# State products of three weight chunks in two row halves of the array, the first two reads in column groups, and a late store issued by ScalarE

## The chip, the cores and the metric

The kernel runs on one core of one Trainium2 chip. The metric is the device time of one execution in microseconds (us), as the median of several runs. The page and the trace come from one profiled execution.

## What is computed

Eight batches of attention against a small state (8 heads, 512 tokens, 32 state rows, width 64) are followed by two feed-forward layers. Cut to what matters:

```python
scores = x @ state.T / 8                 # a = softmax over the 32 state rows
xread  = softmax(scores, -1) @ state     # 512 rows for each batch and head
sread  = softmax(scores.T, -1) @ x       # 32 rows for each batch and head
x = concat(xread, sread)                 # 8 x (512 + 32) rows of width 512
g = relu(x @ w_in) ** 2                  # w_in 512 x 2048
x = g @ w_out                            # w_out 2048 x 512
h = x @ w2_in                            # then h * softmax(h), a layer norm, and @ w2_out
```

Everything is worked out in float32 to about its precision. A factor is split into a high and a low part, both in 32 bits, and a product is three matmuls: high by high, high by low, low by high.

## The kernel before

`xread` is never formed for the first layer. Since xread @ w_in = softmax @ (state @ w_in), the kernel forms **state products**: for each batch the rows state @ w_in (32 state rows of 8 heads, in four chunks of 512 columns of w_in). The hidden layer of a batch is then softmax times those rows (`hidden`, two triples of matmuls for 128 hidden columns), `project` accumulates the second product in four PSUM banks, and ScalarE and VectorE square and split between them.

The state products come in three kinds. Chunk 0 of batches 0 and 1 goes straight from PSUM into a tile (`sw_direct`). Chunk 0 of batches 2 and 3, and chunks 1 to 3 of batches 0 to 3, are made by `sw_part(u, j)`: u is chunk times 4 plus the pair of heads, j the pair of batches. Its weights hold one head of two batches, in `bdw` for j = 0 and `bd` for j = 1; the other head's rows of these 128 rows are zeros, so a pair of heads and two batches fill 128 columns, and three matmuls make them (`triple`, lines 149 to 151 of the profile). ScalarE copies the bank out (L347), and SyncE (SP) stores it to DRAM. `late_part` does batches 4 to 7 later (L417 and L418), with the copy L419 on ScalarE and the store L421 in SP's queue. `load_sw` fetches the rows back.

The **reads** (`sread` in the reference) are small matmuls in plain float32, each of which the trace shows as two passes. For batches 0 and 1, `sread` takes x as weights, 64 columns wide, and moves 32 columns (L651), and ScalarE puts the result into the tile `sr`. From batch 2 on `read_four` takes the softmax as weights, 32 columns wide, in four column groups of the array and moves 64 columns (L673); VectorE transposes the result (`tq`), which goes through DRAM into `sr`.

What sets the order: up to the 28th hidden block (about the first 170 us) the order of TensorE, VectorE, ScalarE and SP is a list written out by hand, `PLAN`. A letter names a kind of work and each time a name stands there one step of it is issued: W is `sw_part`, F the first reads, U a step of the state's transposes, H, G, L and P the parts of the feed-forward. GpSimd follows its own order. After that `step` places the work block by block (16 blocks for a batch), with tables `tensor`, `scalar`, `vector` and `after` for the attention of the batch after next, and a table `EARLY` at the turn to the second layer. All PSUM banks of `ps_m` (two, for transposes, scores and most state products) and of `ps_h` (two, for `hidden`) are taken in turn.

## Time and profile before

| | |
|---|---|
| Median of 3 runs | 1025.05 us (1024.75 to 1026.1) |
| The profiled execution's own time | 1025.25 us |
| Its span, first to last instruction | 1023.5 us |
| TensorE busy | 1007.6 us (98%) |
| VectorE busy | 780.6 us (76%) |
| ScalarE busy | 624.1 us (61%) |
| GpSimd busy | 135.4 us (13%) |

A timeline row gives an instruction's start, its duration, engine, line, output, inputs and shape, and in brackets the idle time of its engine before it with what ended it. A matmul's duration holds its way through the array, so the pace of TensorE is read from start to start and not from durations.

### The profile page before, as it was taken

How to read it: one execution, taken by the hardware profiler on the slowest of the kernel's cores; microseconds unless marked ns; L12 is line 12 of the kernel's file. 1: busy time of each engine (PE TensorE's matmuls, PEld its weight loads, DVE VectorE, ACT ScalarE, POOL GpSimd, SP SyncE). 2: the span in 40 equal slices, each digit the busy share in tenths (PEclk: the TensorE clock that was granted, in tenths of full speed). 3: DMA queues.
4: the chain of work that ended last, by engine and by line, in shares of the span. 5: the costliest groups of instructions: out<-in, count | busy, mean ns of one | idle time of the engine just before them, and what ended most of it. 6: DMA issues, size and time to landing. Idle time of an engine off the chain costs nothing.

```text
span 1023.5 us, 14984 instructions
## 1 busy us (share of the span) xinstructions
PE 1007.6 (98%) x5118; PEld 837.4 (82%) x5118; DVE 780.6 (76%) x1383; ACT 624.1 (61%) x1047; POOL 135.4 (13%) x170
## 2 busy tenths in 40 slices
PE   6999999999999999999999999999999999999998
PEld 4788888888888878888888889998888888888887
DVE  7999889788677588697796455699788788778861
ACT  6998776466566555465564443476756666666652
POOL 1000000001000000010000023322422332232010
PEclk9999999999999999999999999999999999999999
DMA  9788976687787773543542726444355445444431
GB/s 250 294 251 266 303 241 205 195 231 200 220 233 221 205 206 106 157 119 113 150 114 90 214 62 203 147 144 160 130 177 166 141 152 177 155 139 159 154 114 53
DMA packets 193837, 179.53 MB, mean 175 GB/s; under 512 B 103008, under 2 KB 142944, under 8 KB 193760
## 3 DMA queue, kind: packets, MB, share of 16 engines
q1 hardware_dynamic: 193040, 178.31, 57.1%
q8 instruction: 40, 0.66, 0.2%
q14 instruction: 37, 0.30, 0.1%
q10 hardware_dynamic: 720, 0.26, 0.1%
HBM read 109.45 MB, written 69.07 MB: 174 GB/s over the span
## 4 chain that ended last, share of the span: by engine, by line
PE 90%; DVE 4%; ACT 2%; DMA 2%; issue 1%; SPq 0%; ACTq 0%; DVEq 0%
PE b L1065 14%; PE acc L149 11%; PE acc L150 11%; PE acc L151 11%; PE ps_h L149 6%; PE ps_h L150 6%; PE ps_h L151 6%; PE ps_o L1208 6%; PE ps_o L1207 6%; PE ps_o L1206 6%; PE ps_sw L418 1%; PE ps_sw L417 1%; PE ps_sr L673 1%; DMA a_st<-in_state_dram 1%; DMA st<-in_moe_w_out_dram 1%
## 5 line engine op out<-in xcount | busy, mean ns | idle before, releaser
L149 PE MATMUL acc<-gh,w1out 128*128 128x512 f32 (+1 forms) x576 | 219.0, 380 | 0.0
L150 PE MATMUL acc<-gl,w1out 128*128 128x512 f32 (+1 forms) x576 | 217.6, 378 | 0.0
L151 PE MATMUL acc<-gh,w1out 128*128 128x512 f32 (+1 forms) x576 | 217.5, 378 | 0.0
L907 ACT ACTIVATE r<-ps_h 128x512 f32<-128x512 f32 (+1 forms) x144 | 82.5, 573 | 127.4 <-PE ps_h L151 124.9
L922 DVE TENSOR_TENSOR gl<-r,gh 128x512 fp32r<-128x512 f32 (+1 forms) x144 | 97.9, 680 | 55.3 <-ACT gh L917 49.0
L917 ACT ACTIVATE gh<-r 128x512 fp32r<-128x512 f32 (+1 forms) x144 | 87.3, 606 | 70.4 <-DVE r L911 64.0
L151 PEld LDWEIGHTS acc<-gh,w1out 128*128 128x128 f32 x576 | 108.4, 188 | 20.2
L149 PEld LDWEIGHTS acc<-gh,w1out 128*128 128x128 f32 x576 | 108.4, 188 | 20.2
L150 PEld LDWEIGHTS acc<-gl,w1out 128*128 128x128 f32 x576 | 108.4, 188 | 19.8 <-DVE gl L922 0.2
L911 DVE TENSOR_TENSOR r<-r,ps_h 128x512 f32<-128x512 f32 (+1 forms) x120 | 77.6, 646 | 45.0 <-ACT r L907 43.8
L1208 PE MATMUL ps_o<-w,ll 128*128 128x512 f32 x272 | 106.0, 390 | 0.3 <-DVE s L1121 0.3
L1206 PE MATMUL ps_o<-w,lh 128*128 128x512 f32 x272 | 106.0, 390 | 0.0
L1207 PE MATMUL ps_o<-w,lh 128*128 128x512 f32 x272 | 105.8, 389 | 0.0
L149 PE MATMUL ps_h<-ah,sw 128*128 128x512 f32 x256 | 100.1, 391 | 0.0
L150 PE MATMUL ps_h<-al,sw 128*128 128x512 f32 x256 | 99.7, 389 | 0.0
L151 PE MATMUL ps_h<-ah,sw 128*128 128x512 f32 x256 | 99.6, 389 | 0.0
L209 POOL TENSOR_TENSOR cw<-cw,ce 128x512 f32<-128x512 f32 x16 | 20.7, 1295 | 493.0 <-DVE ce L206 409.4
L1065 PE MATMUL b<-w,x2h 128*128 128x512 f32 x272 | 83.9, 390 | 0.0
L1138 POOL TENSOR_TENSOR var<-var,mhalf 128x1 f32<-128x1 f32 x34 | 35.1, 1032 | 247.3 <-DVE var L1137 247.3
L1181 ACT ACTIVATE lh<-ln_t 128x1024 fp32r<-128x1024 f32 x32 | 33.8, 1055 | 46.8 <-PE ps_o L1207 45.1
L1208 PEld LDWEIGHTS ps_o<-w,ll 128*128 128x128 f32 x272 | 51.0, 188 | 11.3 <-DVE ll L1187 0.7
L1206 PEld LDWEIGHTS ps_o<-w,lh 128*128 128x128 f32 x272 | 51.1, 188 | 10.6
(246 smaller groups left out, 2031.2 us busy)
## 6 DMA issues: line engine op xcount, KB each, us to landing
ln_d<-ln_sq SPq DMA_DIRECT2D x32, 512.0 KB, 3.4
ln_t<-ln_d SPq DMA_DIRECT2D x128, 128.0 KB, 2.9
stg<-sw_d SPq DMA_DIRECT2D x120, 128.0 KB, 3.5
sw_d<-ev_sw SPq DMA_DIRECT2D x28, 512.0 KB, 3.9
st<-in_moe_w_out_dram SPq DMA_DIRECT2D x24, 512.0 KB, 4.8
st_x<-x_d SPq DMA_DIRECT2D x34, 256.0 KB, 3.6
w1i_d<-w1in SPq DMA_DIRECT2D x16, 512.0 KB, 5.7
st<-in_moe_w_in_dram SPq DMA_DIRECT2D x16, 512.0 KB, 5.2
```

What stands on the lines that cost most here:

```text
L149: nc.tensor.matmul(out=ps, lhsT=lh, rhs=rh, start=first and i == 0, stop=False)
L150: nc.tensor.matmul(out=ps, lhsT=lh, rhs=rl, start=False, stop=False)
L151: nc.tensor.matmul(out=ps, lhsT=ll, rhs=rh, start=False, stop=last and i == n - 1)
L907: nc.scalar.activation(out=r, in_=ps, func=AF.Relu)
L911: nc.vector.tensor_tensor(out=r, in0=r, in1=ps, op=ALU.mult)
L917: nc.scalar.activation(out=gh, in_=r, func=AF.Copy if times else AF.Square)
L922: nc.vector.tensor_tensor(out=gl, in0=r, in1=gh.bitcast(F32), op=ALU.subtract)
L1065: nc.tensor.matmul(out=ps, lhsT=l, rhs=r, start=first and k == 0 and j == 0, stop=k == 1 and j == 2, skip_group_check=True,)
L1138: nc.gpsimd.tensor_tensor(out=var, in0=var, in1=mhalf, op=ALU.pow)
L1206: nc.tensor.matmul(out=ps, lhsT=a, rhs=wt[:, 0, o : o + 512], start=(k == 0), stop=False)
L1207: nc.tensor.matmul(out=ps, lhsT=a, rhs=wt[:, 1, o : o + 512], start=False, stop=False)
L1208: nc.tensor.matmul(out=ps, lhsT=bb, rhs=wt[:, 0, o : o + 512], start=False, stop=(k == NK - 1))
```

## The change

Three edits of substance, with the orders written anew around them.

First, for chunks 1 to 3 a new `sw_rows` makes the products of one pair of heads for all four batches. A new tile `stw` holds the state of one head in partitions 0 to 63 and of the other head in 64 to 127, four batches in 128 columns. Two matmuls of 64 rows, one in each row half of the array, go to two PSUM banks, one of `ps_m` and one of `ps_h`; three such pairs make the product. Sixteen copies by GpSimd fill `stw` from `bdw` and `bd`. Chunk 0 of batches 2 and 3 stays as it was, and is stored in two pieces. The stores go to one tensor `sw1_d` in place of four. `stw` uses the buffer of `sr`, which is taken later.

Second, batches 0 and 1 are read by `read_four` too, through the transpose and DRAM.

Third, the store of `late_part` is issued by ScalarE.

Beside that: `PLAN` is another list; the columns' softmax of batches 3 to 7 and the reads of all batches from 2 on stand one step earlier; the fetched softmax uses the buffers `xh` and `xl`; the entry 22 of `EARLY` puts `part_hi` ahead of `sol_square`.

```diff
+    stw = srp.tile([P, 2, NQ, 2, 2, 2 * NS], F32R, tag="sr", name="stw")
...
+        if t > 1:
+            return
+        for l in range(2):
+            o, n = slice(l * D, (l + 1) * D), slice(l * NS, (l + 1) * NS)
+            for i in range(2):
+                for lo in range(2):
+                    nc.gpsimd.tensor_copy(
+                        out=stw[o, lo, :, i, t].rearrange("p q (n b) -> p q n b", b=2),
+                        in_=half(i, lo)[o, :, n, :],
+                    )
...
+        if c:
+            yield from sw_rows(c, hp, t)
+            return
...
+    def sw_rows(c, hp, t):
+
+        q, i = divmod(hp, 2)
+        pss = [bank("ps_sw"), ps_h.tile([P, 512], F32, tag="h", name="ps_sw")]
+        for n, (lo, r) in enumerate(((0, 0), (0, 1), (1, 0))):
+            for l in range(2):
+                o = slice(l * D, (l + 1) * D)
+                nc.tensor.matmul(
+                    out=pss[l],
+                    lhsT=stw[o, lo, q, i].rearrange("p j r -> p (j r)"),
+                    rhs=t[o, r, :],
+                    start=(n == 0),
+                    stop=(n == 2),
+                    tile_position=(l * D, 0),
+                )
+        ev = evp.tile([P, 2, 512], F32, tag="ev", name="ev_sw")
+        for l in range(2):
+            yield 1
+            nc.scalar.activation(out=ev[:, l, :], in_=pss[l], func=AF.Copy)
+        yield 1
+        nc.sync.dma_start(out=sw1_d[:, 2 * hp : 2 * hp + 2, c * FC : (c + 1) * FC], in_=ev)
...
         if i == 1:
-            nc.sync.dma_start(out=sw2_d[:, 2 * k : 2 * k + 2, c * FC : (c + 1) * FC], in_=ev)
+            nc.scalar.dma_start(out=sw2_d[:, 2 * k : 2 * k + 2, c * FC : (c + 1) * FC], in_=ev)
...
+        def read_four(i):
...
+            for t in range(NT):
+                for hp in range(NHP):
+                    h = 2 * hp + i
+                    nc.tensor.matmul(
+                        out=v["ps_sr"][hp * NS : (hp + 1) * NS, i * D : (i + 1) * D],
+                        lhsT=col_of(t, h),
+                        rhs=xs_t[b][:, t, h, :] if b < 2 else xs[:, h // 4, t, h % 4, :],
...
+                        tile_position=(0, hp * NS),
+                    )
...
-        after = {14: [(read_four,), (read_turn,)]}
+        after = {13: [(read_four, 0), (read_four, 1), (read_turn,)]}
...
-    I2 i2 I0 X0 i2 U0 i0 U0 i2 X0 i0 i2 X0 U0 i0 i0 i2 X0 T02 T03 i0 i0 T00 J0 J2 i2 U0 T02 N02 i2 T03 T00
+    I2 I0 X0 X0 X0 X0 i2 J0 i0 U0 i0 U0 T02 T03 i0 i0 i0 i2 i2 J2 i0 U0 T02 i0 i2 T03 X1 U0 i2 T00 N02 i0 X1
...
-        22: ([(sol_square, 2, "A")], [(part_hi, 1, "A"), (part_lo, 1, "A"), (sol_mul, 2, "B"), (load_pair, 5)]),
+        22: ([(part_hi, 1, "A")], [(part_lo, 1, "A"), (sol_square, 2, "A"), (sol_mul, 2, "B"), (load_pair, 5)]),
```

TensorE at the first products of chunk 1. Before, one product of a pair of heads is two triples, each into a bank of its own; `bdw_221` holds batches 0 and 1, `bd1_1_204` batches 2 and 3.

```order
L149 MATMUL ps_sw_697<-w1in_605,bdw_221 128x512
L150 MATMUL ps_sw_697<-w1in_605,bdw_221 128x512
L151 MATMUL ps_sw_697<-w1in_605,bdw_221 128x512
L149 MATMUL ps_sw_708<-w1in_605,bd1_1_204 128x512
L150 MATMUL ps_sw_708<-w1in_605,bd1_1_204 128x512
L151 MATMUL ps_sw_708<-w1in_605,bd1_1_204 128x512
L149 MATMUL acc3_713<-gh_616,w1out_382 128x512
```

TensorE at the first product of chunk 1 now: the two banks alternate, and the rows of `project` stand on either side.

```order
L402 MATMUL ps_sd_634<-sw_690,negi_199 128x512
L372 MATMUL ps_sw_701<-w1in_434,stw_206 128x512
L372 MATMUL ps_sw_702<-w1in_434,stw_206 128x512
L372 MATMUL ps_sw_701<-w1in_434,stw_206 128x512
L372 MATMUL ps_sw_702<-w1in_434,stw_206 128x512
L372 MATMUL ps_sw_701<-w1in_434,stw_206 128x512
L372 MATMUL ps_sw_702<-w1in_434,stw_206 128x512
L156 MATMUL acc2_712<-gh_667,w1out_386 128x512
```

Six rows stay six, with half the rows of the array each, and they make what six made before.

SP before, at a store of `late_part` (`sw2_d`) between loads of x for the attention (`xs`), of a late product's weights (`w1in`) and of state products (`stg`):

```order
L517 DMA xs_208<-in_x_dram 32x16x32 x8
L274 DMA w2_d3_69<-cw_3877 128x512
L401 DMA w1in_4097<-w1i_d3_65 64x2x512 x2
L421 DMA sw2_d_61<-ev_sw_4132 128x2x512
L439 DMA stg_4148<-sw2_d_61 32x2x512 x4
L687 DMA sr_d4_125<-tq_3989 128x128
```

SP now at the same place, without the store:

```order
L546 DMA xs_207<-in_x_dram 32x16x32 x8
L281 DMA w2_d3_66<-cw_3909 128x512
L434 DMA w1in_4129<-w1i_d3_62 64x2x512 x2
L469 DMA stg_4180<-sw2_d_58 32x2x512 x4
L693 DMA sr_d4_124<-tq_3976 128x128
```

The store now stands on ScalarE, behind the two copies that fill its tile and ahead of the next blocks' squares:

```order
L920 ACTIVATE r_3767<-ps_h_3751 128x512
L452 ACTIVATE ev_sw_3778<-ps_sw_3779 128x512
L452 ACTIVATE ev_sw_3778<-ps_sw_3786 128x512
L454 DMA sw2_d_58<-ev_sw_3778 128x2x512
L930 ACTIVATE gh_3799<-r_3767 128x512
L920 ACTIVATE r_3821<-ps_h_3801 128x512
```

One entry has left SP's queue and joined ScalarE's, at each of the 16 late products.

ScalarE before at entry 22 of `EARLY`: the square `hA,var` stands ahead of the high part `lh` of a row of the second layer's input to w2_out.

```order
L1086 ACTIVATE s_7620<-b_7610 128x512
L1131 ACTIVATE hA,var<-e,mu 128x1024
L1181 ACTIVATE lh<-ln_t 128x1024
L1219 ACTIVATE ob<-ps_o 128x512
L1131 ACTIVATE hB,var<-e,mu 128x1024
```

ScalarE there now:

```order
L1099 ACTIVATE s_7652<-b_7642 128x512
L1194 ACTIVATE lh<-ln_t 128x1024
L1144 ACTIVATE hA,var<-e,mu 128x1024
L1232 ACTIVATE ob<-ps_o 128x512
L1144 ACTIVATE hB,var<-e,mu 128x1024
```

The square has moved behind the high part, and nothing else has moved there.

## Rows read from the trace of the kernel before

**Rows 1.** The page: span, and busy time with share of each engine.

```profile
span 1023.5 us, 14984 instructions
PE 1007.6 (98%) x5118; PEld 837.4 (82%) x5118; DVE 780.6 (76%) x1383; ACT 624.1 (61%) x1047; POOL 135.4 (13%) x170
```

**Rows 2.** Who waited for whom: total us, times, longest us.

```profile
ACT r L907 <- PE ps_h L151: 124.9, 102, 2.8
...
PE ps_st L305 <- DMA a_st<-in_state_dram: 8.9, 1, 8.9
...
PE ps_s L738 <- ACT ev_sw L419: 1.0, 2, 0.8
```

**Rows 3.** Busy time in two stretches: us of each engine (instructions), clock, DMA.

```profile
25.00:77.00 52.00, 51.45 (x297) 41.55 (x296) 50.61 (x111) 49.34 (x98) 2.10 (x2) 1.00 0.81 273
25.00:170.00 145.00, 144.00 (x763) 117.65 (x762) 132.17 (x270) 122.58 (x234) 2.10 (x2) 1.00 0.82 261
```

**Rows 4.** Instructions on the tile ps_sw: ns least/median/most, first and last start, form.

```profile
L347 ACT ACTIVATE ev_sw<-ps_sw x28: 578/597/678, 32.0 to 142.7; 128x512 f32<-128x512 f32 x28
L149 PEld LDWEIGHTS ps_sw<-w1in,bd x16: 186/188/190, 28.2 to 136.3; 128*128 128x128 f32 x16
L149 PE MATMUL ps_sw<-w1in,bd x16: 389/391/507, 28.4 to 136.6; 128*128 128x512 f32 x16
...
L149 PE MATMUL ps_sw<-w1in,bdw x12: 389/389/496, 43.0 to 139.3; 128*128 128x512 f32 x12
```

**Rows 5.** Timeline of TensorE: a product's first matmul and the one behind it.

```profile
58.61 0.39 PE L149 MATMUL ps_sw<-w1in,bdw 128*128 128x512 f32 x1
...
59.29 0.39 PE L149 MATMUL acc<-gh,w1out 128*128 128x512 f32 x1
```

**Rows 6.** Timeline of TensorE: matmuls of 256 columns, ten apart.

```profile
629.77 0.28 PE L149 MATMUL ps_h<-sh,w1in 128*128 128x256 f32 x1
...
630.98 0.28 PE L150 MATMUL ps_h<-sl,w1in 128*128 128x256 f32 x1
```

**Rows 7.** Timeline of TensorE around reads of batch 0, and a half of batch 1.

```profile
69.36 0.40 PE L151 MATMUL acc<-gh,w1out 128*128 128x512 f32 x1
69.69 2.06 PE L651 MATMUL ps_sr<-e,xs 128*64 128x32 f32 x64
...
72.01 0.39 PE L150 MATMUL ps_sw<-w1in,bdw 128*128 128x512 f32 x1
...
111.55 0.39 PE L151 MATMUL ps_h<-ah,sw 128*128 128x512 f32 x1
...
113.26 0.39 PE L150 MATMUL acc<-gl,w1out 128*128 128x512 f32 x1
```

**Rows 8.** Timeline of TensorE around the read of batch 2, in column groups.

```profile
194.92 0.39 PE L151 MATMUL ps_h<-ah,sw 128*128 128x512 f32 x1
195.24 1.10 PE L673 MATMUL ps_sr<-xs,e 128*32 128x64 f32 x64
...
196.61 0.40 PE L150 MATMUL acc<-gl,w1out 128*128 128x512 f32 x1
```

**Rows 9.** Timeline of TensorE at two of its few waits.

```profile
361.59 0.39 PE L151 MATMUL acc<-gh,w1out 128*128 128x512 f32 x1
362.76 0.50 PE L738 MATMUL ps_s<-xh,bd 128*128 128x512 f32 x1 [0.78 <-ACT ev_sw L419]
...
714.18 0.39 PE L1207 MATMUL ps_o<-w,lh 128*128 128x512 f32 x1
714.89 0.50 PE L1208 MATMUL ps_o<-w,ll 128*128 128x512 f32 x1 [0.32 <-DVE s L1121]
```

**Rows 10.** Timeline of VectorE just ahead of the second of these waits.

```profile
713.61 1.22 DVE L1187 TENSOR_TENSOR ll<-ln_t,lh 128x1024 fp32r<-128x1024 f32 x1 [0.73 <-ACT lh L1181]
```

**Rows 11.** Timeline of ScalarE's queue: two DMAs that it issues.

```profile
2.32 1.21 ACTq L294 DMA_DIRECT2D a_st<-in_state_dram  x2
```

**Rows 12.** Timeline of GpSimd: the first of its two early products.

```profile
27.09 1.05 POOL L607 TENSOR_TENSOR e<-e,sm 128x512 f32<-128x512 f32 x1 [22.46 <-DVE sm L605]
```

More of the change, by code (lines that the diff above doesn't have):

```diff
@@ L56, in memory_attention_relu2_solu @@
     dram = ctx.enter_context(tc.tile_pool(name="dram", bufs=1, space=DRAM))
-    sw_d = [dram.tile([P, B // 4, F1], F32, name=f"sw_d{hp}", tag=f"sw{hp}") for hp in range(NHP)]
+    sw1_d = dram.tile([P, H, F1], F32, name="sw1_d", tag="sw1")
     sw2_d = dram.tile([P, H, F1], F32, name="sw2_d", tag="sw2")
@@ L69, in memory_attention_relu2_solu @@
     st_d = [dram.tile([P, 2, S], F32, name=f"st_d{b}", tag=f"st{b}") for b in range(2, B)]
-    sr_d = [dram.tile([P, P], F32, name=f"sr_d{b}", tag=f"sr{b}") for b in range(2, B)]
+    sr_d = [dram.tile([P, P], F32, name=f"sr_d{b}", tag=f"sr{b}") for b in range(B)]
     x2p_d = [dram.tile([P, NM, S], F32, name=f"x2p_d{b}", tag=f"x2p_{b}") for b in range(2)]
@@ L120, in memory_attention_relu2_solu, with sr_tile @@
     bdw = {}
-    sr = srp.tile([P, NHP, NSR], F32, tag="sr", name="sr")
+    stw = srp.tile([P, 2, NQ, 2, 2, 2 * NS], F32R, tag="sr", name="stw")
+    srt = []
+    def sr_tile():
+        if not srt:
+            srt.append(srp.tile([P, NHP, NSR], F32, tag="sr", name="sr"))
+        return srt[0]
     def split(hi, lo, src):
@@ L329, in sw_part @@
         c, hp = divmod(u, NM)
-        i = hp % 2
-        single = c == 0
-        at = i if single else j
-        ps = ps_h.tile([P, 512], F32, tag="h", name="ps_sw") if u < AHEAD else bank("ps_sw")
-        if j == 0:
-            lh, ll = (bdw[0][:, i, hp // 2, k] for k in (i, 2 + i))
-        else:
-            lh, ll = (bd[i][j][:, hp // 2, k] for k in (i, 1 - i))
-        lh, ll = lh.rearrange("p n b -> p (n b)"), ll.rearrange("p n b -> p (n b)")
-        t = w1u[u]
+        q, i = divmod(hp, 2)
@@ L341, in sw_part @@
+        t = w1u[u]
+        if c:
+            yield from sw_rows(c, hp, t)
+            return
+        ps = ps_h.tile([P, 512], F32, tag="h", name="ps_sw")
+        lh, ll = (bd[i][j][:, q, k].rearrange("p n b -> p (n b)") for k in (i, 1 - i))
         triple(ps, [(lh, ll, t[:, 0, :], t[:, 1, :])], True, True)
         yield 1
-        key = (hp // 2, j) if single else u
-        if key not in sw_ev:
-            sw_ev[key] = evp.tile([P, 2, 512], F32, tag="ev", name="ev_sw")
-        ev = sw_ev[key]
@@ L347, in sw_part @@
-        nc.scalar.activation(out=ev[:, at, :], in_=ps, func=AF.Copy)
-        yield 1
-        if single:
-            nc.sync.dma_start(out=sw_d[hp][:, j, c * FC : (c + 1) * FC], in_=ev[:, at, :])
-        elif j == 1:
-            nc.sync.dma_start(out=sw_d[hp][:, j - 1 : j + 1, c * FC : (c + 1) * FC], in_=ev)
+        if q not in sw_ev:
+            sw_ev[q] = evp.tile([P, 2, 512], F32, tag="ev", name="ev_sw")
+        ev = sw_ev[q]
+        nc.scalar.activation(out=ev[:, i, :], in_=ps, func=AF.Copy)
@@ L429, in load_sw @@
         if b < B // 2:
[L430 to L435 removed]
+            o = b // 2 * D + b % 2
+            rows = sw1_d[o : o + D - 1 : 2]
         else:
             r = (b - B // 2) * NS
[L438 to L442 removed]
+            rows = sw2_d[r : r + NS]
+        for h in range(4):
+            nc.sync.dma_start(
+                out=st[h * NS : (h + 1) * NS], in_=rows[:, h::4, c * FC : (c + 1) * FC]
+            )
         loading[b, c] = st
@@ L1498, in step @@
                 load_sw(*chunks[i])
[L1499 to L1500 removed]
+        if ws in (3, 5) and rows_of.get(w):
+            rows_of[w].pop(0)()
+        if w == 2 and ws in (7, 9):
+            rows_of[(ws - 7) // 2].pop(0)()
         if ws in (0, 1) and 2 <= w < B - 1:
```

155 lines of the change are left out of this document (62 added, 93 removed).

## The prediction, made before the changed kernel was run

> **What bounds the kernel now.** I read the page first, then the waits, then two stretches of the part that the hand-written order covers, then single rows. The page: TensorE is busy for 1007.6 of 1023.5 us, 98%, and the next engine, VectorE, for 76% [rows 1]. The waits: TensorE's only long one is 8.9 us for the state at the start, which the change does not touch, and the next is 1.0 us [rows 2]. So the end is TensorE's sum of work, and time removed from its queue shortens the kernel if the others keep up. That condition is not free everywhere. From 25 to 77 us VectorE is busy for 50.6 and ScalarE for 49.3 of 52 us; from 25 to 170 us, where all state products of chunks 1 to 3 lie [rows 4], VectorE for 132.2 and ScalarE for 122.6 of 145 us [rows 3]. The granted clock is 1.00 there, its upper level of 2.4 GHz.
>
> **Part 1, the state products.** Before, chunks 1 to 3 take 3 x 4 pairs of heads x 2 pairs of batches = 24 triples; with chunk 0's four the rows show 16 + 12 = 28 [rows 4]. From the first matmul of a triple to what follows the third it is 59.29 - 58.61 = 0.68 us [rows 5], 0.227 for one. A pair of heads costs 6 x 0.227 = 1.36 us, and there are 12.
>
> Now the same six instructions have 64 rows each, two at a time in different halves of the array. No row of this trace shows two row halves at work. The nearest is the read of batch 2: four column groups, 64 passes of 64 columns in 1.10 us [rows 8], where at the pace of 256 columns in 0.121 us [rows 6] they would take 64 x 0.030 = 1.9 us one after the other. Passes in different column groups overlap, so I take it that row halves do. The price of a pair I bound from two sides: 0.227 if the second half costs nothing, 0.454 if nothing overlaps. I take 0.24, two matmuls of 256 columns with their own weight loads at (630.98 - 629.77) / 10 = 0.121 [rows 6], since a pair too must load two sets of weights in the time.
>
> Going into another partition of the array and back costs something too. Batch 0's reads together, 72.01 - 69.36 = 2.65 us less two ordinary matmuls (0.45), cost 2.20; half of batch 1's alone costs 113.26 - 111.55 - 0.45 = 1.26, two halves 2.51 [rows 7]. The same work split in two excursions costs 0.31 more: that is the price of one. For row halves it is bounded by 0 and 0.31 unless the weight loads come out from behind the matmuls, which is a rival below; I take the measured 0.31.
>
> One product is then 3 x 0.24 + 0.31 = 1.03 us instead of 1.36, 0.33 less, and 12 give **-3.9 us** (from -8.2, with 0.227 and no excursion, to +4.0, with no overlap: 6 x 0.227 + 0.31 = 1.67).
>
> ScalarE makes as many copies of products as before: 4 + 24. SP's stores of chunk 0 become eight for four. Sixteen GpSimd copies of 64 x 128 elements come in: by GpSimd's 1.05 us for 128 columns x 4 of two inputs [rows 12] a quarter is 0.26, at most 1.05. They stand before and between the two early products of GpSimd, on which the first transposes of batch 0 wait. Six stand between these two; at 0.26 that is 1.6 us, which VectorE's own work before the second product covers in part. That goes into part 4.
>
> **Part 2, the first reads.** Batches 0 and 1 cost 2.20 + 2.51 = 4.71 us on TensorE. A read in the new form costs 196.61 - 194.92 - 0.45 = 1.24 us [rows 8], two 2.48: **-2.2 us**. Batch 1's now stands right behind a state product and may save half an excursion (-2.4). VectorE gets two transposes of the result and ScalarE loses two copies; SP gets two stores and two sets of four fetches, needed only by the last block of the first layer. All lie beside TensorE's work.
>
> **Part 3, the later stages.** TensorE waited twice for a copy of a late state product, 1.0 us in all [rows 2]; the first of these, from matmul to matmul, is 362.76 - 361.59 = 1.17 us for 0.23 [rows 9]. ScalarE was late there because it waited for VectorE, which had waited for loads of x. SP's queue loses a store that waited for a copy ahead of such loads, and the reads release the buffer of x a step earlier. I count two thirds of the 1.0, **-0.7 us** (0 to -1.3). The store costs ScalarE an issue: two took 1.21 us [rows 11], so 0.6 each, 9.7 us over 16. It is hidden by ScalarE's waits for TensorE, 124.9 us over 102 squares [rows 2], 1.2 each; behind it in the queue stand the next block's squares. Uncovered it would cost up to 9.7 us, and is part of the third rival.
>
> At entry 22 of EARLY TensorE lost 714.89 - 714.18 - 0.23 = 0.48 us to a low part [rows 9], for which VectorE had waited 0.73 us on ScalarE's high part [rows 10]. With the square behind the high part this is up to 1.1 us earlier: **-0.5 us**. A product's pair to column softmax, its exp and its copies only change their step.
>
> **Part 4, the hand-written order with less TensorE work.** Parts 1 and 2 take 6.1 us out of a stretch in which VectorE has 145 - 132.2 = 12.8 us left [rows 3]. Fitted into 138.9 us its work is 95%; from 25 to 77 us it stands at 97% already. What comes late there cannot all be made up by other blocks' matmuls. I take **+1.5 us** for it, GpSimd's copies included, a quarter of what is gained there (bounds 0 and all of it, 6.1). What is late next is VectorE's low parts, for which `project` waits.
>
> **The sum.** -3.9 - 2.2 - 0.7 - 0.5 + 1.5 = -5.8 us against the profiled execution's own 1025.25 us: 1019.45. The median of the runs is 0.2 below that execution, so I forecast **1019.2 us**. With the better bounds throughout (-8.2, -2.4, -1.8, 0) it would be 1012.7.
>
> **A rule against the change.** The rows show that a full matmul's weight load, 0.188 us [rows 4], costs nothing at a pace of 0.227 [rows 5], though it goes into the rows in which the matmul ahead still runs. The Trainium skill, "TensorE: Matmul & The Clock Gate", section "The mechanism" of Part 3, says that a weight load overlaps with matmuls in flight only where its row group is another one; with both halves at work none is free. By that rule alone the loads of each pair would come out, and the first rival's second price would hold; the full matmuls above do not obey it, and the rest of the argument does not use it.
>
> **Rivals.**
>
> *The halves do not overlap, so the change does not do what it says.* Either the two matmuls of a pair follow each other, +4.0 for part 1, or each pair waits for its weights, 3 x (0.24 + 0.188) + 0.31 = 1.59 instead of 1.36, +2.8. The stretch is then not shorter, or only by part 2, so part 4 is nothing: 1025.05 + 4.0 - 3.4 = 1025.7, or 1024.5. For it speaks that no row shows row halves; against it the overlap of column groups [rows 8].
>
> *VectorE sets the end of the first 170 us.* If its share cannot rise over the 91% of now, parts 1 and 2 gain nothing: 1025.05 - 1.2 = 1023.9; with half of them, 1020.8. For it speak the 97% and the 95% for ScalarE [rows 3]; against it that TensorE scarcely waits in the same stretch now [rows 2].
>
> *Slower: two banks at once.* A product now takes a bank of each pool, and both come free only after two copies by ScalarE of 0.6 us each [rows 4] in a queue that is 95% full. The next score or hidden block then stands where TensorE stood at 362 us, 1.17 - 0.23 = 0.94 us [rows 9]. At 12 products that is 11.3 us: 1030.5. It makes the kernel slower from 0.66 us for each, (1027.1 - 1019.2) / 12. Against it: 28 copies had to be made in the same queue before without a wait of TensorE, and behind most products the new order puts matmuls of `project`, which need no new bank.
>
> **How the numbers follow.** About 0.2% (2 us) is what a measurement of this kernel can tell from no change: faster is under 1023.0, slower over 1027.1. The forecast and its spread, 0.60; better than its lower end, 0.03; VectorE the bound, 0.15 (two thirds of it still faster); no overlap, 0.14, half for each of its two prices (same but for a little); two banks or another new wait, 0.08. Faster is 0.60 + 0.03 + 0.10 = 0.73; same 0.05 + 0.13 = 0.18; slower 0.08 + 0.01 = 0.09. The range runs from 1014.0, near the better bounds, to 1024.8, which takes in the second rival and the waiting weights: 0.60 + 0.15 + 0.07 = 0.82.
>
> **What would show it.** Overlap: the six rows of a product start two at a time, and from the first to what follows the last is near 1.0 us; 1.6 means no overlap. Reads: two of 1.2 us in place of 4.7 in all. Part 3: no wait of scores for late copies, no gap at entry 22. Part 4: TensorE's waits up to 170 us grow by about 1.5 us, on VectorE. The prediction is wrong if the products are at 1.0 us and the time is still at 1025 (then the second or the third rival, by the releaser named in the waits), or if the gain lies in stages that parts 1 to 4 do not name.

## The result: slower by 1.2%, and the profile after

The changed kernel takes 1038.59 us (median of 4 runs, 1037.57 to 1039.38) against 1025.41 us of the kernel before: ratio 1.0122, 95% interval 1.0108 to 1.0137. That is 13.2 us slower where 6 us faster was forecast, outside the range. The profiled execution took 1039.19 us, its span is 1037.4.

The page of the changed kernel (busy time and share of the span) and the two stretches (us of each engine, granted clock, DMA share, GB/s) answer to [rows 1, 3]:

```profile
span 1037.4 us, 15017 instructions
PE 1010.2 (97%) x5118; PEld 829.9 (80%) x5118; DVE 781.2 (75%) x1385; ACT 624.7 (60%) x1045; POOL 143.4 (14%) x186
```

```profile
25.00:77.00 52.00, 47.23 (x211) 34.20 (x210) 45.71 (x99) 45.45 (x89) 5.72 (x10) 0.93 0.70 236
25.00:170.00 145.00, 138.25 (x740) 104.20 (x739) 128.78 (x263) 120.31 (x229) 5.72 (x10) 0.98 0.81 254
```

From 25 to 170 us TensorE, VectorE and ScalarE do less than before, VectorE 128.8 us where it did 132.2; GpSimd's 3.6 us more are copies into `stw`. So none of the three has become full: they wait more (TensorE's 5.8 us less also hold the work that the change took from it). TensorE's waits (total us, times, longest) answer to [rows 2]:

```profile
PE ps_s L744 <- ACT ev_sw L452: 3.7, 3, 1.8
PE ps_a L147 <- POOL e L636: 1.8, 1, 1.8
PE ps_x L147 <- DMA xs<-in_x_dram: 1.5, 1, 1.5
PE ps_sw L450 <- DMA w1in<-w1i_d: 1.4, 2, 1.1
```

The wait for a late copy is 3.7 us instead of 1.0, the one for x 1.5 us instead of 0.4, and new ones stand beside them: for GpSimd's product and for a load of w1. Where the time goes is seen best from one mark that both programs have, the first matmul of each triple of the hidden layer (256 in all, two for a hidden block). Blocks stand at other places among the other work now, so that single marks move by some us either way. The rows are TensorE's on the tile ps_h in 30 to 50 us (ns least/median/most, first and last start); the first is of the kernel before, the second of the changed one:

```profile
L149 PE MATMUL ps_h<-ah,sw x8: 389/389/476, 36.0 to 47.8; 128*128 128x512 f32 x8
```

```profile
L156 PE MATMUL ps_h<-ah,sw x4: 389/393/497, 44.9 to 48.6; 128*128 128x512 f32 x4
```

The first stands at 44.9 us instead of 36.0 (at 41.3 in e3 below, which runs the same program). Some of this is made up by 160 us, where the 48th is 5.5 us late; up to 320 us it falls behind again, to 14.9 us at the 112th, and 14 us stay to the end. In this execution TensorE's granted clock was 0.57 from 36 to 44 us, so mostly the lower of the two levels (1.2 GHz), after it had waited 1.8 us for GpSimd; in e3 below, which has the same order on every engine, it was 1.00 there, so the median need not rest on that. The stretch in the changed kernel and in e3:

```profile
36.00:44.00 8.00, 7.31 (x25) 5.36 (x23) 4.39 (x12) 6.23 (x12) 0.48 (x2) 0.57 0.03 13
```

```profile
36.00:44.00 8.00, 7.23 (x34) 5.39 (x33) 6.46 (x16) 7.90 (x16) 0.00 (x0) 1.00 0.25 59
```

The parts that the change is about do what was forecast. A read of batch 0 and a product in row halves, TensorE's timeline (they answer to [rows 7] and [rows 5]):

```profile
80.91 0.40 PE L158 MATMUL acc<-gh,w1out 128*128 128x512 f32 x1
81.24 1.10 PE L679 MATMUL ps_sr<-xs,e 128*32 128x64 f32 x64
82.27 0.50 PE L156 MATMUL acc<-gh,w1out 128*128 128x512 f32 x1
82.61 0.40 PE L157 MATMUL acc<-gl,w1out 128*128 128x512 f32 x1
...
98.51 0.39 PE L158 MATMUL ps_h<-ah,sw 128*128 128x512 f32 x1
98.83 0.97 PE L372 MATMUL ps_sw<-w1in,stw 64*128 64x512 f32 x6
99.73 0.50 PE L156 MATMUL acc<-gh,w1out 128*128 128x512 f32 x1
100.06 0.40 PE L157 MATMUL acc<-gl,w1out 128*128 128x512 f32 x1
```

The product costs 100.06 - 98.51 = 1.55 less two ordinary matmuls (0.45), 1.10 us (1.36 before, 1.03 forecast), the read 82.61 - 80.91 = 1.70 less the same, 1.25 us (1.24 forecast).

### The profile page after: what moved, and what is told of

Its sections match the earlier page's. It is cut to its first block, busy times and chain, and to the rows that moved or that the text cites. A ratio compares the mean times of both kernels' runs of the same rounds, so it can differ in the third digit from the quotient of the medians.

```text
span 1037.4 us, 15017 instructions
## 1 busy us (share of the span) xinstructions
PE 1010.2 (97%) x5118; PEld 829.9 (80%) x5118; DVE 781.2 (75%) x1385; ACT 624.7 (60%) x1045; POOL 143.4 (14%) x186
## 4 chain that ended last, share of the span: by engine, by line
PE 87%; DMA 6%; ACT 2%; SPq 2%; DVE 2%; issue 1%; POOL 0%; ACTq 0%; DVEq 0%; POOLq 0%
PE b L1078 16%; PE acc L156 11%; PE acc L157 10%; PE acc L158 10%; PE ps_o L1221 6%; PE ps_o L1220 6%; PE ps_o L1219 6%; PE ps_h L156 6%; PE ps_h L158 6%; PE ps_h L157 6%; DMA sw_d<-ev_sw 2%; DMA stg<-sw_d 1%; DMA st64w<-in_moe_w_in_dram 1%; PE ps_sw L372 1%; DMA st<-in_moe_w_out_dram 1%
```

## The experiments

"Ratio" is to the kernel before on the same chip, with its 95% interval. The main kernels as a table; "old" and "new" mean as in the kernel before and as in the changed one:

| kernel | products, reads | order | late store | moved steps | x packets | ratio |
|---|---|---|---|---|---|---|
| changed | new | new | ScalarE | new | 128 B | 1.0122 |
| e1 | new | new | SP | new | 128 B | 1.0086 |
| e10 | new | new | SP | old | 128 B | 1.0064 |
| e7 | old | new | SP | old | 128 B | 1.0064 |
| e17 | new | new | SP | old | 2 KB | 0.9988 |
| e11 | new | new behind an old start | SP | old | 128 B | 1.0051 |
| e20 | new | new behind an old start | SP | old | 2 KB | 0.9960 |
| e19 | old | old | SP | old | 2 KB | 0.9982 |
| e13 | new | old | SP | old | 128 B | 1.0104 |

e11, e13 and e20 also have the second half of GpSimd's copies behind both of its early products.

### The late store on ScalarE (e1, e2)

e1 undoes it in the changed kernel, e2 makes it alone in the kernel before:

```diff
-            nc.scalar.dma_start(out=sw2_d[...], in_=ev)
+            nc.sync.dma_start(out=sw2_d[...], in_=ev)
```

Expected of e1: 

> The changed kernel with one edit: the sixteen late stores of state products go back from ScalarE's queue to SP's, as in the kernel before. Theory A (the late store costs the time after 200 us): DMAs share eight completion semaphores in turn, so a load on SP eight places behind a store on ScalarE waits until that store has landed (3.6 us). In the trace of the changed kernel SP waits 14.1 us for it before stores, and 9.3, 6.6 and 6.4 us before loads. Then the loss between 180 and 420 us (6.4 us more than before, by progress of TensorE) goes away: 1038.6 - 6.4 = 1032.2, from 1031 to 1033.5, and SP's waits for the landing are gone. Rival B (the moved steps of reads and column softmax cost that stretch, not the store): 1038.6 within 1 us, the waits of scores at 232 us stay.

Expected of e2: 

> The kernel before with one edit: its sixteen late stores are issued by ScalarE instead of SP. Theory A (shared completion semaphores hold SP's loads back): slower by 4 to 8 us, about 1031.5, with TensorE's new waits between 200 and 420 us behind loads of low parts or of w1 that came late. The prediction's own view (the issue is hidden, SP's queue is relieved): faster by 0.3 to 0.7, about 1024.9. Rival B (the store matters only together with the moved steps): 1025.4 within 1 us.

Measured: e1 1033.76 us, ratio 1.0086 (1.0066 to 1.0106), 3.7 us less than the changed kernel by the ratios; e2 1030.22 us, 1.0049 (1.0031 to 1.0067), 5.0 us more than the kernel before. Theory A holds, though e1 gains a little less than it said; the prediction's "hidden, and SP relieved" falls. SP's waits in the changed kernel from 180 to 420 us:

```profile
SPq L546 <- DMA sw_d<-ev_sw: 14.1, 3, 6.7
SPq L434 <- DMA sw_d<-ev_sw: 9.3, 2, 4.8
SPq L531 <- DMA sw_d<-ev_sw: 6.6, 3, 3.0
SPq L829 <- DMA sw_d<-ev_sw: 6.4, 2, 3.4
```

SP waits for the *landing* of a store that it has not issued and whose data these loads (of x, of w1 and, L829, of the softmax) do not read; in e1 0.3 us is left of these 36. The semaphore numbers in the trace's DMA records show why. The 820 DMAs of both queues together carry eight completion semaphores, 102 to 109, in turn, in the order in which the program is written; none of the 812 that have one of the same number before them starts before that one, eight places ahead, has landed. One place of the changed kernel, as timelines of SP, of ScalarE and of TensorE:

```profile
215.53 8.09 SPq L546 DMA_DIRECT2D xs<-in_x_dram  x4
223.66 1.24 SPq L434 DMA_DIRECT2D w1in<-w1i_d  x2
224.94 2.00 SPq L469 DMA_DIRECT2D stg<-sw_d  x4
```

```profile
219.93 0.40 ACTq L454 DMA_DIRECT2D sw_d<-ev_sw  x1
...
230.85 0.63 ACT L492 ACTIVATE sw<-stg 128x512 fp32r<-128x512 f32 x1 [3.89 <-DMA stg<-sw_d]
232.54 1.06 ACT L452 ACTIVATE ev_sw<-ps_sw 128x512 f32<-128x512 f32 x2
```

```profile
228.79 0.47 PE L450 MATMUL ps_sw<-w1in,st_t 128*128 128x512 f32 x1 [1.10 <-DMA w1in<-w1i_d]
...
233.17 0.51 PE L744 MATMUL ps_s<-xh,bd 128*128 128x512 f32 x1 [1.82 <-ACT ev_sw L452]
```

ScalarE issues the store at 219.93, with semaphore 105, behind a copy that waited for TensorE's product; it lands at 223.29. SP's fourth load of x has its place eight behind it, 105 again, and starts at 223.31; everything behind it in SP's queue, w1 and the states of the next block, is late, ScalarE sits 3.89 us for these states, its copies are late, and TensorE waits twice, for w1 and for the copies. The issue itself costs ScalarE 0.40 us, less than the 0.6 of [rows 11]. The Trainium skill says ("DMA: Bandwidth & Descriptors", section "Issuing engines are not separate DMA queues") that issuing from several engines saves only the time that the sequencer takes to issue. In this trace it also cost: it tied SP's queue to the progress of ScalarE.

### The moved steps (e10, e15)

e10 puts them back (on top of e1), e15 makes them alone in the kernel before, both with the buffer of the fetched softmax that goes with them:

```diff
-        after = {13: [(read_four, 0), (read_four, 1), (read_turn,)]}
+        after = {14: [(read_four, 0), (read_four, 1), (read_turn,)]}
...
-            scalar[7].append((col_exp, 1))
...
-            vector[10].append((col_turn, 1))
+            vector[10].append((col_turn, 0))
+            vector[11].append((col_turn, 1))
+            after |= {11: [(col_fetch, 0)], 12: [(col_fetch, 1)]}
```

Expected of e10: 

> The changed kernel with the late store on SP again and, as one edit more, the steps of read and column softmax of batches 3 to 7 in their old places (the read behind block 14, the column steps one or two blocks later, their buffer the old one). To compare with the run that has only the store on SP (ratio to before 1.0086). Theory F (the moved steps make ScalarE's copies of late products late: in that run scores wait 2.3 us at 300 us and 2.1 us at 380 us for them, in the kernel before 1.0 us): these waits fall to about 1 us in all and the time by 3 to 5 us, ratio 1.004 to 1.006. Rival G (these waits come from the shifted phase between the hand-written part and the rest): ratio within 0.001 of 1.0086.

Expected of e15: 

> The kernel before with one edit: reads of batches 2 to 7 one block earlier and the column softmax steps of batches 3 to 7 in their new places, with the new buffer. Theory F (the moved steps put ScalarE's copies of late products late): TensorE's waits for such a copy grow from 1.0 us to 2 to 4 us, the time by 1 to 3 us, ratio 1.001 to 1.003. The prediction counted these moves as nothing or a gain of part of 0.7 us: ratio 0.9995 to 1.000.

Measured: e10 1.0064 (1.0049 to 1.0079), 2.3 us below e1, with intervals that overlap; e15 1.0031 (1.0018 to 1.0045), 3.2 us. So the moves cost some 2 to 3 us. In e15's profiled execution 1.7 of its 3.1 us are there at the first hidden block already, ahead of any moved step, and 1.4 us come behind 190 us, where the steps have moved; so the size is less sure than the sign. The scores' wait for late copies in 180 to 420 us is 4.4 us in e1, 2.9 in e10, 2.2 in e15 (1.0 in the kernel before), in this order:

```profile
PE ps_s L744 <- ACT ev_sw L452: 4.4, 2, 2.3
```

```profile
PE ps_s L744 <- ACT ev_sw L452: 2.9, 2, 1.9
```

```profile
PE ps_s L738 <- ACT ev_sw L419: 2.2, 3, 1.0
```

That is theory F's sign: in e15 at its upper size, in e10 under the 3 to 5 us that it expected, with waits of 2.9 us instead of 1. Which of the moved steps does it was not taken apart.

### GpSimd's copies (e3, e8)

Expected of e3: 

> The changed kernel with one edit: the eight GpSimd copies of the second pair of batches are issued later, in front of the third store of chunk 0's third pair of heads, behind both early GpSimd products; the first state product of chunk 1 comes some 12 us after that. Theory C (six copies of 0.42 us between the two products make the first transposes of batch 0 wait, and TensorE's clock falls after that wait): the second product ends 2.5 us earlier, TensorE's wait of 1.8 us at 35 us goes, the granted clock stays at the upper level, about 3.3 us more: 1038.6 - 5 = 1033.5, from 1032 to 1035. Rival D (the new order itself is late there, whatever GpSimd does): within 1 us of 1038.6, the first hidden block still starts at 45 us instead of 36.

GpSimd's order is not written by hand, so issuing the copies later in the program changed nothing in it: every engine has the same instructions in the same order, and e3 is the changed kernel over again (1.0124, 1.0103 to 1.0144). It tells nothing of theories C and D. e8 makes GpSimd's queue follow the written order:

```diff
-    by_hand = {... for e in ("PE", "DVE", "Activation", "SP")}
+    by_hand = {... for e in ("PE", "DVE", "Activation", "SP", "Pool")}
...
+            if p == "W21" and later:
+                later.pop()()
```

Expected of e8: 

> The changed kernel with GpSimd's queue also in written order, and the eight copies of the second pair of batches issued behind both early GpSimd products (in the changed kernel six stand between them). Theory C (these copies cost): the second product ends about 2.5 us earlier, TensorE's wait of 1.8 us for it at 35 us shrinks to the 0.7 us that the kernel before with the new order shows there, and the time falls by 1 to 2.5 us, to about 1036.8. Theory D (the order itself costs the start, and the next late step is right behind): no more than 0.5 us is gained.

Measured: 1.0106 (1.0090 to 1.0123), 1.6 us below the changed kernel, with intervals that overlap. The timelines of GpSimd, changed kernel and e8:

```profile
30.46 1.05 POOL L636 TENSOR_TENSOR e<-e,sm 128x512 f32<-128x512 f32 x1 [14.28 <-ACT bd L324]
31.45 2.51 POOL L336 CAST stw<-bd 64x128 fp32r<-64x128 f32 x6
34.04 1.37 POOL L636 TENSOR_TENSOR e<-e,sm 128x512 f32<-128x512 f32 x1
```

```profile
28.70 1.05 POOL L644 TENSOR_TENSOR e<-e,sm 128x512 f32<-128x512 f32 x1 [10.79 <-DVE sm L642]
30.41 1.05 POOL L644 TENSOR_TENSOR e<-e,sm 128x512 f32<-128x512 f32 x1 [0.66 <-DVE sm L642]
```

A copy is 2.51 / 6 = 0.42 us, not the 0.26 worked out from [rows 12]. Without six of them ahead the second product ends at 31.5 us instead of 35.4 in the changed kernel's trace and 33.9 in e3's, so 2.5 us earlier than in the better of the two traces with them, and TensorE's wait there falls from 1.8 to 0.7 us, both as theory C said. The gain of 1.6 us is theory C's too, but its interval does not exclude theory D's 0.5.

### The new order (e7, e9, e11)

e7 is the kernel before with the new order, its second product in a bank of the other pool:

```diff
-        ps = ps_h.tile(...) if u < AHEAD else bank("ps_sw")
+        ps = ps_h.tile(...) if u < AHEAD or j == 1 else bank("ps_sw")
...
-    PLAN = (old)
+    PLAN = (new; each product's W tokens for two products)
```

Expected: 

> The kernel before (128-row products, no GpSimd copies, reads as before, late store by SP) with the new hand-written order: both products of a pair of heads stand where the new one stands, the second in the hidden blocks' pool of banks, their copies and the store where the new ones stand. Rival D (the order itself is what costs the start): the first hidden block starts at 43 us or later, and the time is 1025.4 + 6 to 10, about 1033. Theory C (GpSimd's copies are what costs the start): the first hidden block starts at 36 to 39 us and the time is 1025.4 within 3 us; some of it may be lost where the list was laid out for shorter products.

Measured: 1.0064 (1.0048 to 1.0080), 6.6 us. That is theory D's size, with the first hidden block at 40.6 us, between the two theories' marks: the order alone, without row halves or GpSimd copies, costs that much. And e10, which has the new products and reads in the same order, and GpSimd's copies for them, has the same 1.0064: the 5.3 us that TensorE saves there bring nothing on balance.

Expected of e9 (the first 202 steps old, all else as changed): 

> The changed kernel with the first 202 of the 891 steps of the hand-written order as in the kernel before (that is up to the first state product of chunk 1); behind them the remaining steps stand in the new order. Products, reads, late store and moved steps are the changed ones. Theory D (the new order costs 6 to 7 us, most of it before 52 us, since TensorE waits there for loads, GpSimd and copies that the new order puts later): the first hidden block starts at 37 to 38 us, and the time falls by 4 to 6 us, to about 1033.5. Rival E (the loss of the new order lies behind the first products, at 100 to 130 us, or comes from the copies): less than 2 us is gained.

Expected of e11 (the same, with store, steps and copies undone): 

> The changed kernel with all four: old start of the order, late store on SP, old steps, GpSimd copies behind both products. What stays of the change are the products in row halves, the reads in column groups, entry 22, and the new order behind the first 202 steps. If the parts add up (products -3.1, reads -2.2, entry 22 -0.5, and 1 to 2 us lost where old and new order meet): 1025.0 - 5.8 + 1.5 = about 1020.7, ratio 0.996, faster than both kernels. If the gains of TensorE are taken back by other waits wherever they come: ratio 1.000 or more.

Measured: e9 1.0112 (1.0092 to 1.0131); e11 1.0051 (1.0037 to 1.0066), 1031.03 us. e9 gains 1.0 us, less than rival E's 2, and e11 takes the second of its two values. In e11 the first hidden block starts at 36.7 us, nearly as early as before, but by the 16th triple, at 71 us, TensorE is 4.8 us late again. So the late start is not all that holds the stretch, and rival E is nearer. It was not cured by any order that I put together.

### The old order (e12, e13)

Expected of e12: 

> The changed kernel with one edit: the whole hand-written order is the old one; each product in row halves stands where the second of the two old ones stood (the first of them at the first, one 13 and one 18 steps later, where two banks are free), its copies and store at the old places or before. Late store on ScalarE, moved steps, GpSimd copies between the two early products: as changed. Theory I (TensorE's work sets the time; order, store and steps are what costs): 1025.4 - 5.8 + 5 for the store + 2 for the steps = about 1026.6, ratio 1.001. Theory H (in the first 170 us loads and VectorE set the end, so that the shorter products and reads bring nothing there): 1025.4 - 0.5 + 5 + 2 = about 1032, ratio 1.006.

Expected of e13: 

> As the run with the whole old order, and also the late store on SP, the old steps, and GpSimd's copies behind both early products: of the change there stay the products in row halves, the reads in column groups and entry 22. Theory I: 1025.4 - 3.1 - 2.2 - 0.5 = 1019.6, ratio 0.9945. Theory H: 1025.4 - 0.5 and at most 1.5 more, ratio 0.998 to 1.0; VectorE and ScalarE are as busy in 25 to 170 us as before and TensorE waits there by what its work got shorter.

Measured: e12 1.0172 (1.0153 to 1.0191), e13 1.0104 (1.0086 to 1.0122), both worse than with the new order and outside both theories. TensorE's waits in e13 from 40 to 170 us, and the same line in the changed kernel:

```profile
PE ps_h L156 <- ACT ev_sw L391: 6.1, 6, 2.0
```

```profile
PE ps_h L156 <- ACT ev_sw L383: 0.3, 1, 0.3
```

Here the third rival of the prediction comes true: the products, at the places that I gave them, hold two banks, and the next hidden block waits for ScalarE's copies six times. The new order avoids that. It is not a careless list; it pays for two banks at once with other things late.

### Is TensorE the bound at all? (e14, e18)

e14 takes 5.4 us of work from TensorE in the kernel before and moves nothing:

```diff
-        triple(ps, [(lh, ll, t[:, 0, :], t[:, 1, :])], True, True)
+            nc.tensor.matmul(out=ps, lhsT=lh, rhs=t[:, 0, :], start=True, stop=False)
+            nc.tensor.matmul(out=ps, lhsT=lh, rhs=t[:, 1, :], start=False, stop=True)
```

Expected: 

> The kernel before, but each of the 24 state products of chunks 1 to 3 has two of its three matmuls (the one with the low part of the states is left out, so that its output differs): 24 x 0.227 = 5.4 us less for TensorE in the stretch that the change shortens, with nothing else moved. Theory I: 1025.4 - 5.4 = 1020.0, ratio 0.995. Theory H: it falls by less than 2.5 us, ratio above 0.9975, and the waits of TensorE in the first 170 us grow by the rest.

Measured: 0.9987 (0.9973 to 1.0002), 1.3 us for 5.4, by the interval between nothing and a half. That is theory H's side; theory I's 0.995 is excluded. The ten runs spread from 1020.6 to 1027.8 us, and the profiled one, 1021.7, is among the two fastest: in it 3.5 us come through, and TensorE's idle time from 25 to 170 us grows by 1.4 us, so the trace shows less of the new waits than theory H expects. e18 is the part of the change that fits the old order (reads in column groups and entry 22 alone).

Expected: 

> The kernel before with the reads of batches 0 and 1 in column groups (and their way through memory to the last block) and with the change at entry 22, nothing else: 2.2 + 0.5 us less for TensorE. By the prediction's own sum: 1025.4 - 2.7 = 1022.7, ratio 0.9974. By theory H (what TensorE saves in the first 170 us comes through for a quarter, as with two matmuls of three; entry 22 comes through whole): 1025.4 - 0.5 - 0.6 = 1024.3, ratio 0.9989.

Measured: 0.9992 (0.9979 to 1.0004), 0.8 us, not to be told from no change; theory H's 0.9989 is nearer than the prediction's 0.9974.

### VectorE or the loads (e16, e17, e19, e20, e21)

e16 and e17 start from e10. e16 takes one VectorE instruction out of each weight conversion, e17 makes the packets of x larger:

```diff
-        nc.vector.tensor_scalar(out=uu, in0=hi, scalar1=0x1FF, scalar2=None, op0=ALU.bitwise_and)
```

```diff
-    in_=x[b, 2 * hp + i, :, k * 32 : (k + 1) * 32].rearrange("(c r) d -> r c d", r=32),
+    in_=x[b, 2 * hp + i].rearrange("(r c) d -> r (c d)", r=32)[:, k * 512 : (k + 1) * 512]...
```

Expected of e16: 

> The run with the late store on SP and the old steps (ratio to before 1.0064), and in each of the 32 conversions of expert weights one VectorE instruction of 0.42 us less (the mask of the low nine bits is left out, so that the low part of the weights and the output differ): 13 us less for VectorE, nearly all in the first 200 us. Theory J (VectorE is what the first 170 us wait for): TensorE's loss there falls by 5 us or more, ratio 1.002 or less. Theory K (it is the loads, which in this order come 5 to 9 us late for VectorE, that set the end): VectorE only waits longer for words, and the ratio stays within 0.0015 of 1.0064.

Expected of e17: 

> The run with the late store on SP and the old steps (ratio to before 1.0064), and the loads of x by quarters, of the same bytes, take 2 KB from one place per packet instead of 128 B sixteen times (the rows of x land in another order, so that the output differs). Theory K (the loads behind these, of expert weights, come late for VectorE since the DMA engines are 0.9 busy with small packets from 80 to 135 us): VectorE's waits for words fall from 5 to 9 us to under 3 us, ratio 1.003 or less. Theory J (VectorE's own work): within 0.0015 of 1.0064.

Measured: e16 1.0063 (1.0046 to 1.0080), no gain although VectorE has 11.5 us less to do (busy 770.4 us instead of 781.9); e17 0.9988 (0.9976 to 1.0000), 7.8 us less than e10. VectorE's work is not the bound in this order, and the loads of x bear on it: theory K's side. VectorE's waits from 60 to 135 us in e10, e16 and e17, in this order:

```profile
DVE cz L228 <- DMA st<-in_moe_w_in_dram: 4.9, 4, 2.4
DVE cz L228 <- DMA st<-in_moe_w_out_dram: 2.2, 2, 1.2
```

```profile
DVE cz L228 <- DMA st<-in_moe_w_in_dram: 7.8, 4, 3.8
DVE cz L228 <- DMA st<-in_moe_w_out_dram: 1.6, 2, 1.0
```

```profile
DVE cz L228 <- DMA st<-in_moe_w_in_dram: 3.3, 2, 2.1
DVE cz L228 <- DMA st<-in_moe_w_out_dram: 1.5, 2, 0.9
```

The stretch from 100 to 120 us (us of each engine, clock, DMA share, GB/s) in e10, then in e17:

```profile
100.00:120.00 20.00, 17.90 (x80) 13.80 (x79) 16.70 (x34) 14.50 (x28) 0.00 (x0) 1.00 0.96 282
```

```profile
100.00:120.00 20.00, 19.89 (x152) 15.84 (x152) 18.70 (x39) 16.50 (x31) 0.00 (x0) 1.00 0.93 305
```

The DMA packets from 60 to 135 us in e10, then in e17:

```profile
DMA packets 19356, 20.47 MB, mean 273 GB/s; under 512 B 12376, under 2 KB 12504, under 8 KB 19349
```

```profile
DMA packets 11896, 21.14 MB, mean 282 GB/s; under 512 B 4208, under 2 KB 4336, under 8 KB 11888
```

In e10 VectorE waits 7.1 us for raw weights, and the DMA engines are 96% busy from 100 to 120 us while TensorE stands 2.1 us. In e16, with less to do, VectorE waits 9.4 us. With a third of the small packets more bytes pass in the same time, VectorE waits 4.8 us and TensorE almost not. The waits fell less than expected of theory K (to under 3 us), and the time fell more. The Trainium skill ("DMA: Bandwidth & Descriptors", section "Specifications") puts the smallest transfer at full rate at 512 B; the two packet counts agree with it in direction.

So theory K's way, raw weights that come late for VectorE, is not the whole gain. By the marks of the hidden layer e17 is 1.1 us ahead of e10 at the first triple, 3.6 us at the 48th (152 us) and 7.2 us from the 144th (379 us) on: half of the gain comes behind the hand-written order, where e10's TensorE waits 2.9 us for late copies and e17's not at all. The stretch from 300 to 400 us in e10, then in e17:

```profile
300.00:400.00 100.00, 97.10 (x485) 79.36 (x484) 72.55 (x132) 58.55 (x107) 5.18 (x4) 1.00 0.73 204
```

```profile
300.00:400.00 100.00, 100.00 (x501) 82.61 (x500) 77.36 (x141) 59.08 (x107) 6.47 (x5) 1.00 0.67 195
```

And the new order's start is not cured by larger packets: from 25 to 60 us TensorE is idle for 4.0 us in e10 and 4.3 in e17, 0.6 in the kernel before.

Three more tell whose cost that is.

Expected of e19: 

> The kernel before with the x loads by quarters in 2 KB packets, as in the run with larger packets (the rows of x land in another order, so the output differs). It tells how much of that run's gain, 7.8 us, belongs to every kernel with these loads. Theory K (the old order hides these loads, the new one waits for them): only the wait of 1.6 us at 360 to 375 us can go, ratio 0.998 to 1.000. If small packets cost the kernel before as much, ratio 0.993 or less, and the loss of the change is no matter of loads.

Expected of e20: 

> The run with old start of the order, late store on SP, old steps and copies behind both products (ratio 1.0051), with the x loads by quarters in 2 KB packets (output differs). If the loads take back what TensorE saves, the gain that the prediction worked out now shows: 1.0051 - 0.0076 = 0.9975, or 0.9945 if the start is as early as in the kernel before. If something else holds the stretch from 48 to 130 us in this order: above 1.001.

Expected of e21: 

> The changed kernel whole, with the x loads by quarters in 2 KB packets (output differs). If the cost of the late store on ScalarE and of the moved steps comes by way of the x loads too (SP stands with them ahead of loads that other engines wait for): ratio 1.000 or less. If store and steps cost on their own: 1.0122 - 0.0076 = 1.0046.

Measured: e19 0.9982 (0.9973 to 0.9992), 1.8 us: the kernel before pays little for the same packets. In the kernel before VectorE waits 1.2 us for raw weights from 60 to 135 us, at a DMA share of 0.93 from 100 to 120 us (its waits, then its stretch):

```profile
DVE cz L221 <- DMA st<-in_moe_w_out_dram: 1.2, 1, 1.2
```

```profile
100.00:120.00 20.00, 19.89 (x145) 16.30 (x145) 17.58 (x34) 16.11 (x31) 0.00 (x0) 1.00 0.93 292
```

e20 0.9960 (0.9946 to 0.9975), 1020.94 us, between the two values expected: a gain of the change shows once the loads are cheap, but as 2.3 us against e19 (0.9982 - 0.9960), with intervals that just overlap, not as 5.8. e21, the changed kernel with large packets, 1.0057 (1.0038 to 1.0077): store and steps still cost 7 us against e17, so most of their cost does not come by way of the packets.

## Why the prediction was wrong, point by point

**Part 1, the products: right.** The halves overlap; 1.10 us against 1.03, so 12 x 0.26 = 3.1 us of TensorE's work instead of 3.9. The pair was sized right (0.235 us from a product's second pair to its third in the trace's records, 0.24 assumed), the way in and out a little low: 1.10 - 3 x 0.235 = 0.39 us instead of 0.31. (The bound "+4.0" for no overlap should read 12 x 0.31 = 3.7; nothing hangs on it.) The Trainium skill's rule ("TensorE: Matmul & The Clock Gate", section "The mechanism" of Part 3), by which the weight loads of a pair would come out since no row group is free, does not hold here: the six loads of 0.18 us would make it 1.6 us or more. **Part 2, the reads: right**, 1.25 against 1.24 us.

**The first failed step is the premise**: "TensorE's sum of work" is the end, "and time removed from its queue shortens the kernel if the others keep up", with the doubt about the others priced in part 4 at a quarter. e14 measures it: of 5.4 us, 1.3 come through, at most 2.8 by the interval, without any new order. TensorE at 98% did not mean that TensorE alone sets the end. That the old order fits loads, conversions and matmuls to one another, so that they run out together, is a reading that suits this; what holds e14 back was not taken apart. The prediction read VectorE's 97% and ScalarE's 95% in [rows 3] but passed over the last columns of the same rows, the DMA share of 0.81 and 0.82; in the changed order cheaper loads bring 7.8 us (e17) and less work for VectorE none (e16).

**The second is part 4**: "+1.5", with bounds of "0 and all of it, 6.1". The upper bound was wrong in kind: it let the order lose no more than was gained. The order alone costs 6.6 us with the old products (e7), and the gain is lost besides (e10). I had compared the two orders only for what stood beside the products, and not for when the raw weights are loaded and used. Order, products and reads together cost 6.6 us with small packets of x (e10) and 0.6 with large ones (e17 against e19, 0.9988 - 0.9982), so 5.9 us of it hang on these loads, about half of them behind the hand-written order. The 0.6 still hold the 5.8 us that TensorE's work got shorter, so large packets leave some 6 us of other cost; the order alone was not run with them. GpSimd's copies, mis-sized at 0.26 us for 0.42, cost about 1.6 us (e8), not clear of nothing.

**The third is part 3**, "-0.7": it has the wrong sign. The store costs 3.7 to 5.0 us. That SP's queue "loses a store that waited for a copy" was true, but SP now waits for that store's landing, which is later than the copy. The sentence that column steps "only change their step" priced at nothing what costs 2 to 3 us. Entry 22 was right: behind the low part, now without a wait, TensorE's matmuls follow each other, where [rows 9, 10] show the gap (timelines of VectorE and TensorE):

```profile
727.23 1.22 DVE L1200 TENSOR_TENSOR ll<-ln_t,lh 128x1024 fp32r<-128x1024 f32 x1
```

```profile
728.85 0.39 PE L1221 MATMUL ps_o<-w,ll 128*128 128x512 f32 x1
729.08 0.39 PE L1219 MATMUL ps_o<-w,lh 128*128 128x512 f32 x1
```

**The rivals.** "VectorE sets the end of the first 170 us" had the right effect, gains that do not come through, and the wrong engine (e16). "Two banks at once" did not happen in the changed kernel, 0.3 us, but is what happens to these products in the old order, 6.1 us (e13). The third rival also held the store, but as ScalarE's time to issue it (up to 9.7 us) and not as SP's wait for its landing, and the range left this rival out, at a chance of 0.08. No rival had the order as a loss of its own.

**The sum as measured**, in us of 1025.4, from the ratios: store 3.7 (1.0122 - 1.0086), steps 2.3 (1.0086 - 1.0064), what small packets of x cost more than in the kernel before 5.9 (1.0064 - 0.9988, less the 0.0018 that the kernel before gains too), rest 0.6: together 12.5. The rest is a balance: some 6 us of other cost against 5.8 us less work. Of this cost 3.7 us are seen as TensorE's idle time from 25 to 60 us (4.3 in e17, 0.6 in e19). Each term has an uncertainty of 1.5 to 2.5 us from its intervals.

**What stays open.** Which loads in the new order come too late, and whether the DMA engines' share or SP's queue of eight in flight holds them, was not taken apart. Nor was what keeps e20 from the full gain: from 40 to 60 us, where old and new order meet, TensorE is idle for 2.4 us in it and not at all in the kernel before (1.0 us for a low part of VectorE's, 0.7 for a square of ScalarE's, 0.3 for its copies). That the products of chunks 1 to 3 go to one tensor instead of four, and those of chunk 0 in two pieces, was never undone by itself. Of the kernels that leave nothing out and load x in its own order none was measurably faster than the kernel before; the nearest is e18.

## What to carry to other kernels

Before pricing a saving on the busiest engine, take some of its work away in place and time that: in a schedule that is already fitted, the share that comes through (here about a quarter, at most a half) is worth more than any sum of durations. Bound a new order by what it can lose on its own, not by what the edit gains; look in the profile for when loads are issued and who will wait for them. And before a DMA moves to another engine's queue, look at which later DMAs share its completion semaphore: here they waited for its landing.

## What the runs showed of the hardware

- The two matmuls of a pair in row halves start 1 to 45 ns apart in the trace's single records, in ten of the twelve products (in the two others the second one waited). Pairs follow at 0.235 us where it is quickest, full matmuls at 0.227. The rest of the cost is at the edges: 0.32 us from the last full matmul to the first pair (98.51 to 98.83), 0.33 behind the one that follows (99.73 to 100.06).
- A GpSimd copy of 64 x 128 elements from f32 to fp32r takes 0.42 us, against 1.05 us for a product of 128 x 512 of two inputs: a quarter of the columns and half the partitions, and 40% of the time.
- From 60 to 135 us the kernel before has as many packets of under 512 B as e10 (12.3 and 12.4 thousand, among 19.0 and 19.4). Loading the quarters of x in larger ones brought 7.8 us in e10's order and 1.8 in the old one: here the price of small packets depended on the order more than on their number.
- The DMAs that SP and ScalarE issue share eight completion semaphores in turn: of the changed kernel's 820, none of the 812 that have one of the same number before them starts before that one has landed. At most eight are in flight, and a late store in one queue holds loads in the other.
